# Loading the key weights of a projection by contraction rows instead of by column halves

## The chip, the cores and the metric

The kernel runs on one core of a Trainium2 chip. The metric is the device time of one execution in microseconds (us). Executions of one kernel scatter by about 0.4 us to either side. So two things are read side by side: timed runs, compared with runs of the kernel before on the same chip in the same session, and traces, in which the moment when a given matmul starts can be compared to 0.01 us.

## The reference, cut to what matters

```
x = A_x                                  # 2048 tokens x 1024
g = sigmoid((x * gate_w).sum(-1))
a = linear_attention(x, A_wqkv, A_wo)    # q, k, v = x @ A_wqkv; phi(k) = exp(k) or k + 1; ...
b = sliding_window_attention(x, B_wqkv, B_wo)
return g * a + (1 - g) * b
```

Only the first step matters here: the keys of the linear attention, `k = x @ A_wqkv[:, 1024:2048]`, a product of 2048 tokens by 1024 contraction rows by 1024 columns, followed by `phi`.

## The kernel before

The kernel starts with that product. It hands x to TensorE (PE) transposed, in blocks of 128 contraction rows ("a row", kt, from 0 to 7) by 128 tokens ("a tile", t). The transposed blocks are made by transposing DMAs straight from memory, so at the start every matmul waits for two things: a block of x and a block of weights. The sums of four token tiles by two halves of 512 columns are kept in eight tiles of PSUM (`first` below; "the banks" from here on), and the loop goes over the contraction outside, so that work can begin when a part of the rows is there.

```python
WkA = [wpool.tile([P, KT, 512], BF16, name=f"WkA{h}", tag="wa") for h in range(2)]

def load_xT(k, t0, t1):      # two rows, tiles t0 to t1: 128 KB for two tiles, 256 KB for four
    nc.sync.dma_start_transpose(out=xT[:, 2*k:2*k+2, t0*P:t1*P], in_=rows(x, t0*P, t1*P)[:, 2*k*P:(2*k+2)*P])
def load_wk(eng, k, h):      # two rows, half of the columns: 256 KB in pieces of 1 KB
    eng.dma_start(out=WkA[h][:, 2*k:2*k+2, :], in_=A_wqkv[2*k*P:(2*k+2)*P, D+512*h:D+512*h+512] ...)

load_wk(nc.scalar, 0, 0)
load_xT(0, 0, 2)
load_xT(0, 2, 4)
load_wk(nc.sync, 0, 1)
for k in range(1, 4):
    load_wk(nc.sync, k, 0)
    load_xT(k, 0, 4)
    load_wk(nc.sync, k, 1)
for t in range(4, NB):       # the other twelve token tiles
    nc.sync.dma_start_transpose(out=xT[:, :, t*P:(t+1)*P], in_=rows(x, t*P, (t+1)*P))
# ... other weights
WqA = load_w("WqA", A_wqkv, 0, "wa")        # later, into the space of WkA

warm_up(37)                  # matmuls on constants
first = [bank_k(i) for i in range(8)]
for k in range(4):           # pairs of rows
    for half in range(2):
        for t in range(4):
            for kt in (2*k, 2*k+1):
                project(first[4*half+t], t, kt, half)
            if k == 3:       # the bank is complete: ScalarE and VectorE empty it
                phi(work, pk[:, t, half*512:(half+1)*512], first[4*half+t])
for t in range(4, NB): ...   # 16 matmuls per tile, each bank complete after 8
```

The softmax here doesn't subtract the row's maximum and nothing guards it: scores larger than these inputs give would overflow.

Of the kernel before, what the change touches and what calls it, by code (L numbers as in the profile page):

```python
# [10 lines left out]
BF16 = mybir.dt.bfloat16  # L11
# [3 lines left out]
SP = mybir.EngineType.SP  # L15
P = 128
# [23 lines left out]
def kernel(  # L40
# [11 lines left out]
    nc = tc.nc  # L52
    S, D = A_x.shape[1:]
    assert D == 1024 and S == 2048

    x = A_x[0].rearrange("(m two) d -> two m d", two=2)
    out2 = out[0].rearrange("(m two) d -> two m d", two=2)

    def rows(ap, s0, s1):
        return ap[s0 // 1024, s0 % 1024:(s1 - 1) % 1024 + 1, :]  # L60
# [3 lines left out]
    KT = D // P  # L64
# [4 lines left out]

    consts = ctx.enter_context(tc.tile_pool(name="consts", bufs=1))  # L70
    wpool = ctx.enter_context(tc.tile_pool(name="wpool", bufs=2))
    dram = ctx.enter_context(tc.tile_pool(name="dram", bufs=1, space=bass.MemoryType.DRAM))
    big = ctx.enter_context(tc.tile_pool(name="big", bufs=1))
    ps_pj = ctx.enter_context(tc.tile_pool(name="ps_pj", bufs=4, space=bass.MemoryType.PSUM))

    def load_w(name, src, col0, tag, only=(0, 1)):
        halves = []
        for h in only:
            w = wpool.tile([P, KT, 512], BF16, name=f"{name}{h}", tag=tag)
            c0 = col0 + h * 512  # L80
            nc.sync.dma_start(out=w[:], in_=src[:, c0:c0 + 512].rearrange("(kt p) n -> p kt n", p=P))
            halves.append(w)
        return halves

    xT = big.tile([P, KT, S], BF16, name="xT", tag="xT")
    xrow = big.tile([P, NB, D], BF16, name="xrow", tag="vV")

    def load_rows(eng, t0, t1):
        eng.dma_start(out=xrow[:, t0:t1, :], in_=rows(x, t0 * P, t1 * P).rearrange("(t p) d -> p t d", p=P))

    WkA = [wpool.tile([P, KT, 512], BF16, name=f"WkA{h}", tag="wa") for h in range(2)]

    def load_xT(k, t0, t1):
        nc.sync.dma_start_transpose(out=xT[:, 2 * k:2 * k + 2, t0 * P:t1 * P],  # L94
                                    in_=rows(x, t0 * P, t1 * P)[:, 2 * k * P:(2 * k + 2) * P])

    def load_wk(eng, k, h):
        eng.dma_start(out=WkA[h][:, 2 * k:2 * k + 2, :],  # L98
                      in_=A_wqkv[2 * k * P:(2 * k + 2) * P, D + 512 * h:D + 512 * h + 512]
                      .rearrange("(kt p) n -> p kt n", p=P))  # L100

    ones = nc.const_aps.tensor(1.0, [P, P], BF16)
    with tc.manual_schedule(engines={SP}):
        load_wk(nc.scalar, 0, 0)
        load_xT(0, 0, 2)
        load_xT(0, 2, 4)
        load_wk(nc.sync, 0, 1)
        for k in range(1, 4):
            load_wk(nc.sync, k, 0)
            load_xT(k, 0, 4)  # L110
            load_wk(nc.sync, k, 1)
        for t in range(4, NB):
            nc.sync.dma_start_transpose(out=xT[:, :, t * P:(t + 1) * P], in_=rows(x, t * P, (t + 1) * P))
        for t in range(0, NB, 4):
            load_rows(nc.sync, t, t + 4)
        gw_row = consts.tile([P, D], BF16, name="gw_row")
        nc.sync.dma_start(out=gw_row[:], in_=gate_w.partition_broadcast(P))
        WvA = load_w("WvA", A_wqkv, 2 * D, "wb")
        WoA = load_w("WoA", A_wo, 0, "wo")
        WvB = load_w("WvB", B_wqkv, 2 * D, "wc")  # L120
    WqA = load_w("WqA", A_wqkv, 0, "wa")



# [13 lines left out]
    for slot in range(2):  # L138
        nc.gpsimd.memset(qsel[:, slot:slot + 1], 0.0)
        for pair in range(2):  # L140
            r = 64 * pair + 32 * slot
# [9 lines left out]
    def phi(work, dst, pj):  # L151
        e = work.tile([P, 512], F32, name="e", tag="e")
        nc.scalar.activation(out=e[:], in_=pj[:], func=ACT.Exp)  # L153
        nc.vector.tensor_scalar(out=e[:], in0=e[:], scalar1=1.0, scalar2=1e-6, op0=ALU.min, op1=ALU.add)  # L154
        nc.vector.scalar_tensor_tensor(out=dst, in0=pj[:], scalar=0.0, in1=e[:], op0=ALU.max, op1=ALU.add)

    with tc.manual_schedule(engines={PE}):

        with ExitStack() as s1:
# [4 lines left out]
            s1.enter_context(tc.manual_schedule(engines={DVE}))  # L164
            pk = big.tile([P, NB, D], BF16, name="pk", tag="pkO")
            def project(pj, t, kt, half):
                nc.tensor.matmul(pj[:], lhsT=xT[:, kt, t * P:(t + 1) * P], rhs=WkA[half][:, kt, :],  # L167
                                 start=(kt == 0), stop=(kt == KT - 1))

            def warm_up(n):  # L170
# [7 lines left out]
            def bank_k(i):  # L178
                return (ps_1.tile([P, 512], F32, name="pk1_ps", tag="p1") if i & 4 else
                        ps_pj.tile([P, 512], F32, name="pk_ps", tag="pj"))  # L180

            first = [bank_k(i) for i in range(8)]
            for k in range(4):
                for half in range(2):
                    for t in range(4):
                        for kt in (2 * k, 2 * k + 1):
                            project(first[4 * half + t], t, kt, half)
                        if k == 3:
                            phi(work, pk[:, t, half * 512:(half + 1) * 512], first[4 * half + t])
            for t in range(4, NB):  # L190
                for half in range(2):
                    pj = bank_k(2 * t + half)
                    for kt in range(KT):
                        project(pj, t, kt, half)
                    phi(work, pk[:, t, half * 512:(half + 1) * 512], pj)
# [6 lines left out]
            for t in range(1, NB):  # L202
                side.append(lambda t=t: nc.vector.tensor_tensor(
                    out=zacc[:], in0=zacc[:] if t > 1 else pk[:, 0, :], in1=pk[:, t, :], op=ALU.add))
            side.append(lambda: nc.gpsimd.partition_all_reduce(zrow[:], zacc[:], P, bass_isa.ReduceOp.add))
            for t in range(NB):
                side.append(lambda t=t: nc.vector.tensor_tensor_reduce(
                    out=gjunk[:], in0=xrow[:, t, :], in1=gw_row[:], scale=1.0, scalar=0.0, op0=ALU.mult,
# [3 lines left out]
            for half in range(2):  # L212
                g_ = junk.tile([P, KT, 512], BF16, name=f"G{half}", tag=f"G{half}")
                G.append(g_)
                for kt in range(KT):
                    pj = ps_pj.tile([P, 512], F32, name="g_ps", tag="pj")
                    for t in range(NB):
                        nc.tensor.matmul(pj[:], lhsT=xrow[:, t, kt * P:(kt + 1) * P],  # L218
                                         rhs=pk[:, t, half * 512:(half + 1) * 512],
# [12 lines left out]
            for g in range(2):  # L232
                kvp = ps_pj.tile([P, 512], F32, name="kv_ps", tag="pj")[:, 0:256].rearrange("p (c d) -> p c d", c=4)
                for c in range(4):
                    for kt in range(KT):
                        for j in range(2):
                            cols = slice(c * P + 64 * j, c * P + 64 * j + 64)
                            nc.tensor.matmul(kvp[64 * j:64 * j + 64, c, :], lhsT=WvA[g][:, kt, cols],  # L238
                                             rhs=G[g][:, kt, cols], start=(kt == 0), stop=(kt == KT - 1))
# [85 lines left out]
            def qa_units(t, bank, evacuate):  # L325
                def mm(half, kt, st):
                    if kt == 0:
                        st["pj"] = bank()
                    nc.tensor.matmul(st["pj"][:], lhsT=xT[:, kt, t * P:(t + 1) * P], rhs=WqA[half][:, kt, :],  # L329
                                     start=(kt == 0), stop=(kt == KT - 1))  # L330
                    if kt == KT - 1:
                        evacuate(t, half, st["pj"])
                for half in range(2):
                    st = {}
                    for kt in range(KT):
                        yield lambda half=half, kt=kt, st=st: mm(half, kt, st)
# [23 lines left out]
        with ExitStack() as s2:  # L360
# [158 lines left out]
            for c in range(KT):  # L519
                kts[c] = kpool.tile([P, 2, 1024], BF16, name="kt", tag="kt")  # L520
                for hh in range(2):
# [3 lines left out]
                    if 1 <= c <= 2:  # L525
                        t = 2 * (c - 1) + hh
                        nc.sync.dma_start_transpose(out=pqT[0][:, :, t * P:(t + 1) * P],
                                                    in_=pqd[t * P:(t + 1) * P, :])
# [5 lines left out]
            load_wo(1, 0, 8)  # L534
            raw = wpool.tile([P, 4, D], BF16, name="raw", tag="wc")
            fw = wpool.tile([P, 2, D], F32, name="fw", tag="wc")
            lw = wpool.tile([P, 4, D], BF16, name="lw", tag="wa")

            def qa_output(t, half):
                def lhsT(r, kt, j):  # L540
                    return xT[64 * r:64 * r + 64, kt, t * P + 64 * j:t * P + 64 * j + 64]

                def rhs(r, kt):
                    return WqA[half][64 * r:64 * r + 64, kt, :]

                def evacuate(ps, part):
                    if part == 0:
                        nc.scalar.copy(out=raw[:, t - 12, half * 512:(half + 1) * 512], in_=ps[:])
                return lhsT, rhs, evacuate
# [5 lines left out]
        with ExitStack() as s3:  # L555
# [48 lines left out]
            for i, p_ in enumerate(parts):  # L604
# [4 lines left out]
                f = out_part(i, *p_)  # L609
# [33 lines left out]
```

## Time and profile before

| | before |
|---|---|
| median of the first three runs | 473.69 us |
| span of the traced execution | 472.5 us |
| PE busy | 467.8 us (99%) |
| first projection starts | 4.74 us |
| last wait of PE for a load ends | 9.51 us |
| first matmul of the next stage ("G") | 61.32 us |

The page of the profile: the span, PE's busy time, and the chain of work that ended last, followed back from the end.

```profile
span 472.5 us, 13174 instructions
...
PE 467.8 (99%) x5765; PEld 246.4 (52%) x5765; DVE 277.2 (59%) x601; ACT 169.2 (36%) x272; POOL 15.3 (3%) x30
...
PE 97%; DMA 1%; SPq 1%; ACT 0%; issue 0%
```

PE is the bottleneck from end to end: 97% of the chain. All that anything else can win is the time in which PE waits. The timeline of PE shows where that is (start, duration, engine, line, operation, output and inputs, shapes, count, and in brackets the idle time before it with what ended it):

```profile
3.03 1.91 PE L173 MATMUL warm<-const-bfloat16-1.0 128*128 128x128 bf16 x16
4.74 1.10 PE L167 MATMUL pk_ps<-WkA,xT 128*128 128x512 bf16 x4
6.01 2.80 PE L167 MATMUL pk_ps<-WkA,xT 128*128 128x512 bf16 x12 [0.18 <-DMA xT<-in_A_x_dram]
9.51 12.69 PE L167 MATMUL pk_ps<-WkA,xT 128*128 128x512 bf16 x58 [0.69 <-DMA xT<-in_A_x_dram]
```

L173 is the warm-up, L167 the projection. PE waits for a block of x before 6.01 and before 9.51 us, and never again in this stage. Two cautions for reading: the idle time in brackets is too small, because a matmul is drawn as 0.38 us long while the next one starts 0.216 us after it; and the two idle stretches are better taken from the starts of single matmuls, 5.46 to 6.01 and 8.44 to 9.51 us, which is 0.33 and 0.85 us more than 0.216.

The timeline of the sync queue (SP), which issues the loads. A duration here is the time that issuing takes, not the transfer:

```profile
0.80 2.60 SPq L94 DMA_TRANSPOSE xT<-in_A_x_dram  x2
3.45 1.09 SPq L98 DMA_DIRECT2D WkA<-in_A_wqkv_dram  x2
4.58 1.24 SPq L94 DMA_TRANSPOSE xT<-in_A_x_dram  x1
5.87 1.12 SPq L98 DMA_DIRECT2D WkA<-in_A_wqkv_dram  x2
```

The transposes (L94) took 1.30 and 1.24 us to issue at 128 KB and 1.24, 1.73 and 1.24 us at 256 KB (the last two at 7.03 and 9.95 us, after these lines); the loads (L98) 0.46 to 0.59 us. And what the DMA engines moved in each microsecond (the two columns that matter are the last: their busy share, which is the sum of the packets' times and passes 1 where these overlap, and GB/s):

```profile
1.50:2.50 1.00, 1.00 (x13) 1.00 (x10) 0.00 (x0) 0.58 (x1) 0.32 (x3) 1.00 0.35 69
2.50:3.50 1.00, 1.00 (x12) 1.00 (x11) 0.00 (x0) 0.00 (x0) 0.00 (x0) 1.00 1.03 293
3.50:4.50 1.00, 1.00 (x12) 1.00 (x11) 0.00 (x0) 0.00 (x0) 0.00 (x0) 1.00 0.59 133
4.50:5.50 1.00, 1.00 (x9) 0.54 (x6) 0.00 (x0) 0.00 (x0) 0.00 (x0) 1.00 0.74 127
5.50:6.50 1.00, 0.82 (x5) 0.25 (x4) 0.00 (x0) 0.00 (x0) 0.00 (x0) 1.00 1.04 287
6.50:7.50 1.00, 1.00 (x6) 0.44 (x5) 0.00 (x0) 0.00 (x0) 0.00 (x0) 1.00 1.42 266
7.50:8.50 1.00, 1.00 (x7) 0.39 (x4) 0.00 (x0) 0.00 (x0) 0.00 (x0) 1.00 0.94 113
8.50:9.50 1.00, 0.31 (x2) 0.00 (x0) 0.00 (x0) 0.00 (x0) 0.47 (x2) 1.00 1.06 267
```

Between 3.5 and 5.5 us they move 130 GB/s, in the two microseconds after that 266 to 287.

### The profile page before, as it was taken

The numbers are of one execution on the slowest core, as the hardware profiler recorded it, in microseconds if no ns is written. First come the engines' busy times: TensorE is split into PE (matmuls) and PEld (weight loads), VectorE is DVE, ScalarE is ACT, GpSimd is POOL, SyncE is SP. The second block draws the span as 40 slices with busy tenths as digits, with TensorE's granted clock in tenths as the row PEclk, the third lists the DMA queues.
The fourth block names the chain that finished last, engine by engine and source line by source line (L and its number), as shares of the span: only waits on it lengthen the run. The fifth ranks groups of instructions, "written<-read, shape, count | busy, mean of one in ns | idle before, by whom it ended". The sixth has DMA issues, their size and how long they took to land.

```text
span 472.5 us, 13174 instructions
## 1 busy us (share of the span) xinstructions
PE 467.8 (99%) x5765; PEld 246.4 (52%) x5765; DVE 277.2 (59%) x601; ACT 169.2 (36%) x272; POOL 15.3 (3%) x30
## 2 busy tenths in 40 slices
PE   8999999999999999999999999999999999999997
PEld 5444444445444444445666666666665444444444
DVE  0496689990329999999567676767660039900000
ACT  1343321102543333333555555555551134221122
POOL 3300000500000000000000000000000000000000
PEclk9999999999999999999999999999999999999999
DMA  8999980000643233627326526432563853321101
GB/s 196 211 233 378 349 259 0 0 1 0 214 136 105 92 138 132 154 96 244 109 56 104 112 49 94 101 86 59 92 147 83 163 136 76 70 56 45 34 33 46
DMA packets 98780, 55.40 MB, mean 117 GB/s; under 512 B 70178, under 2 KB 90658, under 8 KB 98722
## 3 DMA queue, kind: packets, MB, share of 16 engines
q1 hardware_dynamic: 93554, 50.10, 41.4%
q10 hardware_dynamic: 5168, 4.46, 3.1%
q8 instruction: 45, 0.74, 0.7%
q14 instruction: 13, 0.11, 0.1%
HBM read 26.10 MB, written 15.86 MB: 89 GB/s over the span
## 4 chain that ended last, share of the span: by engine, by line
PE 97%; DMA 1%; SPq 1%; ACT 0%; issue 0%
PE q_ps L387 27%; PE d_ps L584 12%; PE p_ps L293 12%; PE g_ps L218 12%; PE e_ps L584 12%; PE pk_ps L167 11%; PE p_ps L329 9%; PE po L466 2%; PE s2b L444 2%; DMA xT<-in_A_x_dram 1%; SPq L94 1%; PE kv_ps L238 0%; PE w_ps L281 0%; SPq L98 0%; ACT osb L589 0%
## 5 line engine op out<-in xcount | busy, mean ns | idle before, releaser
L387 PE MATMUL q_ps<-xT,WqB 64*64 64x512 bf16 x1024 | 68.3, 377 | 0.0
L387 PE MATMUL q_ps<-xT,WkB 64*64 64x512 bf16 x1024 | 68.0, 377 | 0.0
L154 DVE TENSOR_SCALAR e<-e 128x512 f32<-128x512 f32 x64 | 27.0, 422 | 65.3 <-ACT e L153 65.3
L293 PE MATMUL p_ps<-WvB,xT 128*128 128x512 bf16 x256 | 57.7, 379 | 0.0
L167 PE MATMUL pk_ps<-WkA,xT 128*128 128x512 bf16 x256 | 55.9, 379 | 0.9 <-DMA xT<-in_A_x_dram 0.9
L218 PE MATMUL g_ps<-pk,xrow 128*128 128x512 bf16 x256 | 55.4, 379 | 0.0
L449 ACT ACTIVATE PT<-s2b 128x928 bf16<-128x928 f32 (+4 forms) x40 | 34.2, 854 | 45.5 <-PE s2b L444 45.5
L451 DVE TENSOR_TENSOR PT<-PT,mask 128x928 bf16<-128x928 bf16 (+4 forms) x40 | 23.6, 590 | 38.2 <-ACT PT L449 38.2
L329 PE MATMUL p_ps<-WqA,xT 128*128 128x512 bf16 x192 | 43.4, 379 | 0.0
L584 PEld LDWEIGHTS <-pqT 128*128 128x128 bf16 x272 | 26.0, 98 | 29.8 <-issue 0.4
L584 PEld LDWEIGHTS <-OBT 128*128 128x128 bf16 x272 | 26.0, 98 | 29.4
L167 PEld LDWEIGHTS <-xT 128*128 128x128 bf16 x256 | 24.8, 98 | 31.5 <-DMA xT<-in_A_x_dram 1.9
L218 PEld LDWEIGHTS <-xrow 128*128 128x128 bf16 x256 | 25.0, 98 | 30.2
L293 PEld LDWEIGHTS <-xT 128*128 128x128 bf16 x256 | 24.7, 98 | 30.2 <-issue 0.9
L387 PEld LDWEIGHTS <-WkB 64*64 64x64 bf16 x1024 | 31.9, 107 | 15.2 <-issue 0.4
L387 PEld LDWEIGHTS <-WqB 64*64 64x64 bf16 x1024 | 31.5, 106 | 15.3 <-issue 0.7
L153 ACT ACTIVATE e<-pk_ps 128x512 f32<-128x512 f32 x32 | 18.9, 597 | 41.1 <-PE pk_ps L167 36.9
L298 ACT CAST tmp<-p_ps 128x512 bf16<-128x512 f32 x32 | 18.8, 589 | 35.5 <-PE p_ps L293 30.1
L584 PE MATMUL d_ps<-WoA,pqT 128*128 128x512 bf16 (+1 forms) x136 | 30.9, 370 | 0.0
L584 PE MATMUL d_ps<-WoB,OBT 128*128 128x512 bf16 (+1 forms) x136 | 30.8, 370 | 0.0
L329 PEld LDWEIGHTS <-xT 128*128 128x128 bf16 x192 | 18.8, 98 | 22.6
L584 PE MATMUL e_ps<-WoA,pqT 128*128 128x512 bf16 (+2 forms) x136 | 30.0, 363 | 0.0
(61 smaller groups left out, 486.9 us busy)
## 6 DMA issues: line engine op xcount, KB each, us to landing
vd<-tmp SPq DMA_DIRECT2D x16, 264.0 KB
xrow<-in_A_x_dram SPq DMA_DIRECT2D x4, 1024.0 KB
out_dram<-osb ACTq DMA_DIRECT2D x31, 128.0 KB
pqd<-tmp SPq DMA_DIRECT2D x12, 256.0 KB
WvA<-in_A_wqkv_dram SPq DMA_DIRECT2D x2, 1024.0 KB
WoA<-in_A_wo_dram SPq DMA_DIRECT2D x2, 1024.0 KB
WvB<-in_B_wqkv_dram SPq DMA_DIRECT2D x2, 1024.0 KB
WqA<-in_A_wqkv_dram SPq DMA_DIRECT2D x2, 1024.0 KB
```

The costliest lines, as they stand in the source:

```text
L153: nc.scalar.activation(out=e[:], in_=pj[:], func=ACT.Exp)
L154: nc.vector.tensor_scalar(out=e[:], in0=e[:], scalar1=1.0, scalar2=1e-6, op0=ALU.min, op1=ALU.add)
L167: nc.tensor.matmul(pj[:], lhsT=xT[:, kt, t * P:(t + 1) * P], rhs=WkA[half][:, kt, :], start=(kt == 0), stop=(kt == KT - 1))
L218: nc.tensor.matmul(pj[:], lhsT=xrow[:, t, kt * P:(kt + 1) * P], rhs=pk[:, t, half * 512:(half + 1) * 512], start=(t == 0), stop=(t == NB - 1))
L293: nc.tensor.matmul(st["pj"][:], lhsT=xT[:, kt, t * P:(t + 1) * P], rhs=WvB[half][:, kt, :], start=(kt == 0), stop=(kt == KT - 1))
L298: nc.scalar.copy(out=v[:, half * 16:(half + 1) * 16, 0:Dh], in_=st["pj"][:].rearrange("p (h e) -> p h e", h=16))
L329: nc.tensor.matmul(st["pj"][:], lhsT=xT[:, kt, t * P:(t + 1) * P], rhs=WqA[half][:, kt, :], start=(kt == 0), stop=(kt == KT - 1))
L387: nc.tensor.matmul(banks[o][64 * j:64 * j + 64, :], lhsT=lhsT(r, kt, j), rhs=rhs(r, kt), start=first and kt == 0, stop=kt == KT - 1, skip_ ...
L444: nc.tensor.matmul(s2b[64 * par:64 * par + 64, pair, :, o:o + w], lhsT=kts[c][r, par, k0:k0 + 64], rhs=qz[r, :, par, q0 % 512:q0 % 512 + w ...
L449: nc.scalar.activation(out=pt[:, :, 0:W_], in_=s2b[:].rearrange("p a b s -> p (a b) s")[:, :, 0:W_], func=ACT.Exp, scale=SCALE)
L451: nc.vector.tensor_tensor(out=pt[:, :, 0:W_], in0=pt[:, :, 0:W_], in1=mask[:, None, base:base + W_].broadcast_to([P, 4, W_]), op=ALU.mult)
L584: nc.tensor.matmul(st["ps"][:, 0:n], lhsT=lhsT, rhs=W[c0 // 512][:, c, c0 % 512:c0 % 512 + n], start=(side == 0 and c == 0), stop=(side == ...
```

## The change

Its intent: PE should begin with all four token tiles and both column halves of one row, so that the first 8 matmuls need the least data. The weights are loaded one row at a time over all 1024 columns (256 KB as before, but in pieces of 2 KB), into one tile; rows 0 and 1 have a transpose each (128 KB), the rest go by pairs (256 KB). The groups follow: rows 0 and 1 alone, then pairs. The queue, with what has to be there before PE can go on:

```
position   before                               changed
1 (ACT)    weights rows 0+1, left half          weights row 0
2          x rows 0+1, tiles 0 and 1            x row 0, four tiles
3          x rows 0+1, tiles 2 and 3            weights row 1
4          weights rows 0+1, right half         x row 1
5          weights rows 2+3, left half          weights row 2
6          x rows 2+3    <- PE goes on          x rows 2+3
7          weights rows 2+3, right half         weights row 3  <- PE goes on
```

```diff
-    WkA = [wpool.tile([P, KT, 512], BF16, name=f"WkA{h}", tag="wa") for h in range(2)]
+    WkA = wide.tile([P, KT, D], BF16, name="WkA", tag="wa")       # wide: a new pool with one buffer
-    def load_xT(k, t0, t1): ...
-    def load_wk(eng, k, h): ...
+    def load_xT(kt, n, t0, t1):
+        nc.sync.dma_start_transpose(out=xT[:, kt:kt + n, t0 * P:t1 * P],
+                                    in_=rows(x, t0 * P, t1 * P)[:, kt * P:(kt + n) * P])
+    def load_wk(eng, kt):
+        eng.dma_start(out=WkA[:, kt, :], in_=A_wqkv[kt * P:(kt + 1) * P, D:2 * D])
 ...
+        load_wk(nc.scalar, 0)
+        load_xT(0, 1, 0, 4)
+        load_wk(nc.sync, 1)
+        load_xT(1, 1, 0, 4)
+        for kt in range(2, KT):
+            load_wk(nc.sync, kt)
+            if kt % 2 == 0:
+                load_xT(kt, 2, 0, 4)
 ...
-    WqA = load_w("WqA", A_wqkv, 0, "wa")
+    WqA = wide.tile([P, KT, D], BF16, name="WqA", tag="wa")       # one DMA of 2 MB instead of two
+    nc.sync.dma_start(out=WqA[:], in_=A_wqkv[:, 0:D].rearrange("(kt p) n -> p kt n", p=P))
 ...
-            for k in range(4):
+            for kts_ in ((0,), (1,), (2, 3), (4, 5), (6, 7)):
                 for half in range(2):
                     for t in range(4):
-                        for kt in (2 * k, 2 * k + 1):
+                        for kt in kts_:
                             project(first[4 * half + t], t, kt, half)
-                        if k == 3:
+                        if kts_[-1] == KT - 1:
                             phi(...)
 ... (the later readers of WqA and the tile lw follow suit)
```

More of the change, by code (lines that the diff above doesn't have):

```diff
@@ L71 @@
     wpool = ctx.enter_context(tc.tile_pool(name="wpool", bufs=2))
+    wide = ctx.enter_context(tc.tile_pool(name="wide", bufs=1))
     dram = ctx.enter_context(tc.tile_pool(name="dram", bufs=1, space=bass.MemoryType.DRAM))
@@ L89, in load_rows @@
         eng.dma_start(out=xrow[:, t0:t1, :], in_=rows(x, t0 * P, t1 * P).rearrange("(t p) d -> p t d", p=P))
-    WkA = [wpool.tile([P, KT, 512], BF16, name=f"WkA{h}", tag="wa") for h in range(2)]
-    def load_xT(k, t0, t1):
-        nc.sync.dma_start_transpose(out=xT[:, 2 * k:2 * k + 2, t0 * P:t1 * P],
-                                    in_=rows(x, t0 * P, t1 * P)[:, 2 * k * P:(2 * k + 2) * P])
-    def load_wk(eng, k, h):
-        eng.dma_start(out=WkA[h][:, 2 * k:2 * k + 2, :],
-                      in_=A_wqkv[2 * k * P:(2 * k + 2) * P, D + 512 * h:D + 512 * h + 512]
-                      .rearrange("(kt p) n -> p kt n", p=P))
-    ones = nc.const_aps.tensor(1.0, [P, P], BF16)
-    with tc.manual_schedule(engines={SP}):
-        load_wk(nc.scalar, 0, 0)
-        load_xT(0, 0, 2)
-        load_xT(0, 2, 4)
-        load_wk(nc.sync, 0, 1)
-        for k in range(1, 4):
-            load_wk(nc.sync, k, 0)
-            load_xT(k, 0, 4)
-            load_wk(nc.sync, k, 1)
+    WkA = wide.tile([P, KT, D], BF16, name="WkA", tag="wa")
[4 more added lines that the diff above has]
+        eng.dma_start(out=WkA[:, kt, :], in_=A_wqkv[kt * P:(kt + 1) * P, D:2 * D])
+    ones = nc.const_aps.tensor(1.0, [P, P], BF16)
+    with tc.manual_schedule(engines={SP, mybir.EngineType.Activation}):
+        load_wk(nc.scalar, 0)
[6 more added lines that the diff above has]
+                load_xT(kt, 2, 0, 4)
         for t in range(4, NB):
@@ L166, in project @@
             def project(pj, t, kt, half):
-                nc.tensor.matmul(pj[:], lhsT=xT[:, kt, t * P:(t + 1) * P], rhs=WkA[half][:, kt, :],
+                nc.tensor.matmul(pj[:], lhsT=xT[:, kt, t * P:(t + 1) * P], rhs=WkA[:, kt, half * 512:half * 512 + 512],
                                  start=(kt == 0), stop=(kt == KT - 1))
@@ L328, in mm @@
                         st["pj"] = bank()
-                    nc.tensor.matmul(st["pj"][:], lhsT=xT[:, kt, t * P:(t + 1) * P], rhs=WqA[half][:, kt, :],
+                    nc.tensor.matmul(st["pj"][:], lhsT=xT[:, kt, t * P:(t + 1) * P], rhs=WqA[:, kt, half * 512:half * 512 + 512],
                                      start=(kt == 0), stop=(kt == KT - 1))
@@ L536 @@
             fw = wpool.tile([P, 2, D], F32, name="fw", tag="wc")
-            lw = wpool.tile([P, 4, D], BF16, name="lw", tag="wa")
+            lw = wide.tile([P, 4, D], BF16, name="lw", tag="wa")
             def qa_output(t, half):
@@ L543, in rhs @@
                 def rhs(r, kt):
-                    return WqA[half][64 * r:64 * r + 64, kt, :]
+                    return WqA[64 * r:64 * r + 64, kt, half * 512:half * 512 + 512]
                 def evacuate(ps, part):
```

## The prediction

> What bounds the kernel. The page gives PE busy 467.8 of 472.5 us (99%), and its chain of waits is 97% PE: every stage is a gapless stream of matmuls. The change neither adds nor removes a matmul (the order of instructions on PE, DVE and ACT is the same after the first 64 projections; the queue issues one DMA fewer, the two 1 MB loads of WqA having become one). It can only pay where PE waits, and that is before 9.51 us.
>
> The start, from the timeline and the trace's completion times. Warm-up matmuls run 0.84 to 4.95 us; the first projection starts at 4.74, just after the first transposed block of x landed (4.68). Then PE waits 0.18 us for the second block (landed 5.97) and 0.69 us for the second k-group's block (9.46). From 9.51 on it never waits: 48 matmuls take 10.53 us, 219 ns each, and the 64 projections of the first four tiles end at 20.04. [...] Without any wait the 64 would end at 4.74 + 64 x 0.219 = 18.8. So 1.3 us, 0.27%, is all that can be won.
>
> What the change does there.
> 1. The first block is one row for all four token tiles: 128 KB as before, so it lands at about 4.7 again. The 8 matmuls of row 0 run 4.7 to 6.5 with no wait (0.18 us saved).
> 2. Row 1 needs its weights and a 128 KB block, issued second and third on the queue. Issue costs 1.24 us per transpose and 0.58 per load; I expect the block at 6.2 to 6.5. Row 1 runs to about 8.3.
> 3. Rows 2 and 3 need weight row 3 for their second matmul already, and that load is issued after the 256 KB block. By then 1.5 MB must have arrived; before, PE could go on after 1.25 MB, because half the columns were enough. This is the bill for loading both column halves together. Against it: weight packets double from 1 to 2 KB. Elsewhere in this trace 1 KB packets move at 350 GB/s and 2 KB packets at 390, so 256 KB takes 0.67 instead of 0.75 us [...]. The queue also idles less between 4.5 and 6 us, where it moved some 150 GB/s. Estimate: block at 8.6, weight row 3 at 9.4 (the same position landed at 10.24).
> 4. So PE waits about 1 us in one place, 8.3 to 9.4, then runs through: weight row 5 (estimate 12.2, needed 13.0) and row 7 (15.0, needed 16.5) are in time. The 64 end at about 9.4 + 47 x 0.219 = 19.7, against 20.04.
>
> Gain: 0.3 to 0.4 us. Later parts are off the path: WqA now waits for the last reader of both key halves (about 62 us instead of 60), but is read only beyond 117 us. lw waits for all WqA readers, which end before it is written.
>
> Predicted: 473.3 us, 472.6 to 474.1. Faster by over 2%: 0.5%; within 2%: 99%; slower: 0.5%.
>
> To be seen if right: PE idle about 1 us in one piece around 8.3 to 9.4, released by a WkA load rather than xT; the 64 end at 19.4 to 20; everything later shifted by the same few tenths.
>
> Wrong if: weight row 3 lands at 10.2 as before (then 0.5 us slower), or weight row 5 after 13 us, a second wait; a better fed queue (row 3 by 8.5) would give up to 1.2 us.

(9.4 + 47 x 0.219 = 19.7 us against 20.04, a gain of 0.3 to 0.4 us, is made of numbers from the trace of before and estimates from them.)

## The result, and the profile after

| | before | changed |
|---|---|---|
| median, first comparison (6 runs each) | 473.80 us | 474.14 us |
| ratio | | 1.0007, interval 0.9994 to 1.002 |
| PE goes on for good (second matmul of rows 2 and 3 in the changed kernel) | 9.51 us | 9.86 us |
| first G matmul | 61.32 us | 61.44 us |

Ratios are the mean time of one kernel's fast runs over that of the other's of the same rounds, so they are not quite the ratios of the medians quoted beside them.

The change is not a gain of 0.4 us but, by the medians, a loss of 0.3. The interval of the ratio holds no change too, so the sign rests on the traces, of which e1, e13, e14, e17 and e20 add more. The page and PE's timeline of the changed kernel, to be read against those of before:

```profile
span 472.3 us, 13141 instructions
...
PE 466.3 (99%) x5735; PEld 244.8 (52%) x5765; DVE 277.3 (59%) x601; ACT 169.1 (36%) x272; POOL 15.3 (3%) x30
...
PE 86%; SPq 11%; DMA 2%; issue 1%; ACT 0%
```

```profile
4.74 4.14 PE L167 MATMUL pk_ps<-WkA,xT 128*128 128x512 bf16 x15
9.19 0.39 PE L167 MATMUL pk_ps<-WkA,xT 128*128 128x512 bf16 x1 [0.31 <-DMA xT<-in_A_x_dram]
9.86 12.46 PE L167 MATMUL pk_ps<-WkA,xT 128*128 128x512 bf16 x56 [0.28 <-DMA WkA<-in_A_wqkv_dram]
```

The start is as planned: 16 matmuls of rows 0 and 1 without a wait for data (one of the 16 records is missing). The first four of them start 0.43, 0.43 and 0.32 us apart instead of 0.216, which costs nothing here because PE has to wait afterwards anyway; e8 and e10 come back to it. Then PE waits twice: until 9.19 us for the x block of rows 2 and 3, does a single matmul, and waits until 9.86 for the weights of row 3. From there it runs through. (The chain now shows SPq with 11%. This is no new wait: 30 matmul records are missing, 5735 of 5765, each leaves a false gap in PE, and at one such gap, at 63.17 us, the walk back leaves PE for a load of WvB and goes along the queue. The trace of e1 lacks as many records and has PE at 97%.)

In the changed kernel the 18th matmul starts at 9.86 us, in the kernel before at 9.73. This lag of 0.12 to 0.13 us is still there, unchanged, at the first G matmul. Nothing else in the first 350 us differs between the two traces by more than 0.02 us; near 353 us the trace of before loses 0.2 us more, which is why its span is the longer one all the same.

The sync queue and the DMA engines:

```profile
0.80 1.26 SPq L95 DMA_TRANSPOSE xT<-in_A_x_dram  x1
2.12 0.56 SPq L99 DMA_DIRECT2D WkA<-in_A_wqkv_dram  x1
2.72 1.15 SPq L95 DMA_TRANSPOSE xT<-in_A_x_dram  x1
3.92 0.58 SPq L99 DMA_DIRECT2D WkA<-in_A_wqkv_dram  x1
4.54 1.35 SPq L95 DMA_TRANSPOSE xT<-in_A_x_dram  x1
5.93 1.05 SPq L99 DMA_DIRECT2D WkA<-in_A_wqkv_dram  x2
```

```profile
1.50:2.50 1.00, 1.00 (x13) 1.00 (x11) 0.00 (x0) 0.58 (x1) 0.32 (x3) 1.00 0.60 86
2.50:3.50 1.00, 1.00 (x12) 1.00 (x11) 0.00 (x0) 0.00 (x0) 0.00 (x0) 1.00 1.11 293
3.50:4.50 1.00, 1.00 (x12) 1.00 (x10) 0.00 (x0) 0.00 (x0) 0.00 (x0) 1.00 0.81 137
4.50:5.50 1.00, 1.00 (x7) 0.53 (x5) 0.00 (x0) 0.00 (x0) 0.00 (x0) 1.00 1.21 243
5.50:6.50 1.00, 1.00 (x5) 0.44 (x4) 0.00 (x0) 0.00 (x0) 0.00 (x0) 1.00 0.97 199
6.50:7.50 1.00, 1.00 (x7) 0.47 (x5) 0.00 (x0) 0.00 (x0) 0.00 (x0) 1.00 1.48 187
7.50:8.50 1.00, 0.95 (x6) 0.41 (x5) 0.00 (x0) 0.00 (x0) 0.00 (x0) 1.00 0.95 230
8.50:9.50 1.00, 0.69 (x3) 0.11 (x2) 0.00 (x0) 0.00 (x0) 0.58 (x2) 1.00 1.08 304
```

The sixth DMA of the kernel is issued from 4.54 us (before: 4.58), the seventh from 5.93 (before: 5.87). And from 1.5 to 7.5 us the engines moved 86 + 293 + 137 + 243 + 199 + 187 = 1145 KB (before: 69 + 293 + 133 + 127 + 287 + 266 = 1175 KB). The stretch from 4.5 to 5.5 us was better filled (243 against 127), and the gain was given back in the next two. From 7.5 to 9.5 us the changed kernel did get ahead: 534 KB against 380, so 1679 against 1555 KB in all. The story in two lines: PE now needs the seventh item where it needed the sixth, and the faster arrival that was to pay for it came only in part.

### The profile page after: what moved, and what is told of

Read it like the earlier page. It is cut to its first block, busy times and chain, and to the rows that moved or that the text cites. A ratio compares the mean times of both kernels' runs of the same rounds, so it can differ in the third digit from the quotient of the medians.

```text
span 472.3 us, 13141 instructions
## 1 busy us (share of the span) xinstructions
PE 466.3 (99%) x5735; PEld 244.8 (52%) x5765; DVE 277.3 (59%) x601; ACT 169.1 (36%) x272; POOL 15.3 (3%) x30
## 4 chain that ended last, share of the span: by engine, by line
PE 86%; SPq 11%; DMA 2%; issue 1%; ACT 0%
PE q_ps L387 27%; PE d_ps L584 12%; PE p_ps L293 12%; PE e_ps L584 11%; PE g_ps L218 11%; PE p_ps L329 9%; SPq L112 4%; SPq L82 4%; DMA WvB<-in_B_wqkv_dram 2%; PE po L466 2%; PE s2b L444 2%; SPq L95 1%; SPq L99 1%; SPq L116 1%; SPq L90 0%
## 5 line engine op out<-in xcount | busy, mean ns | idle before, releaser
L584 PEld LDWEIGHTS <-pqT 128*128 128x128 bf16 x272 | 26.0, 98 | 29.8 <-issue 0.4
L584 PE MATMUL e_ps<-WoB,OBT 128*128 128x512 bf16 (+2 forms) x133 | 29.7, 363 | 0.2
```

What stands on the lines that cost most here:

```text
L584: nc.tensor.matmul(st["ps"][:, 0:n], lhsT=lhsT, rhs=W[c0 // 512][:, c, c0 % 512:c0 % 512 + n], start=(side == 0 and c == 0), stop=(side == ...
```

## The experiments

All changes are made in the changed kernel unless said otherwise. "Landed" is the time when the last of a DMA's completion signals was recorded in the trace; "first G matmul" sums up everything that happened in the start. Every kernel gave correct results.

| run | first G matmul, us | x rows 2+3 / weights row 3 landed, us | median us (before beside it) | ratio, 95% interval |
|---|---|---|---|---|
| before | 61.32 | 9.46 / - | 473.80 | |
| changed | 61.44 | 9.14 / 9.82 | 474.14 (473.80) | 1.0007, 0.9994 to 1.002 |
| e1_repeat | 61.67 | 9.00 / 10.05 | 474.68 (473.90) | 1.0014, 1.0002 to 1.0027 |
| e2_single_rows | 61.23 | 8.97 / 10.62 | 473.88 (473.90) | 0.9997, 0.9984 to 1.0009 |
| e3_weights_first | 63.91 | 10.36 / 9.32 | 474.73 (473.90) | 1.0015, 1.0001 to 1.0028 |
| e5_tile_only | 61.34 | 9.48 / - | 473.48 (473.90) | 0.9993, 0.9980 to 1.0006 |
| e4_act_queue | 63.78 | 7.34 / 10.53 | 476.93 (473.79) | 1.0070, 1.0054 to 1.0087 |
| e6_single_all | 61.34 | 8.79 / 10.66 | 473.99 (473.79) | 1.0006, 0.9994 to 1.0018 |
| e8_rows_act | 63.52 | one block per row | 478.58 (473.79) | 1.0098, 1.0071 to 1.0125 |
| e9_short_packets | 61.52 | 9.03 / 9.77 | 474.69 (473.79) | 1.0020, 1.0007 to 1.0033 |
| e10_pair_last | 60.56 | 8.70 / 10.26 | 473.60 (473.66) | 0.9997, 0.9984 to 1.0010 |
| e11_split_block | 61.24 | one block per row | 473.65 (473.66) | 0.9999, 0.9987 to 1.0011 |
| e12_row1_act | 60.89 | 7.63 / 9.16 | 474.56 (473.66) | 1.0018, 1.0002 to 1.0034 |
| e13_before_copy | 61.15 | 9.30 / - | 473.85 (473.41) | 1.0006, 0.9994 to 1.0019 |
| e16_pair_last2 | 60.93 | 8.88 / 10.78 | 473.57 (473.41) | 1.0002, 0.9989 to 1.0016 |
| e14_before_look | 61.15 | 9.29 / - | one run | |
| e17_changed_look | 61.93 | 8.96 / 10.30 | one run | |
| e20_changed_look2 | 61.37 | 9.08 / 9.75 | one run | |
| e18_short_look | 64.42 | 8.84 / 11.11 | one run | |
| e19_short_look2 | 61.65 | 9.15 / 10.03 | one run | |

(For the kernel before, e5, e13 and e14 the first of the two numbers is the block of x of rows 2 and 3, on which PE goes on there. Single runs are used for their traces alone.)

The theory: PE restarts at the seventh item of the queue instead of the sixth, and the queue is no faster. Rivals: the merged tile or the 2 MB load costs something later; the 2 KB pieces are to blame; the transposes hold the weights up.

### e1_repeat: the changed kernel again

No edit.

> The changed kernel again, unaltered. Theory: the change costs 0.1 us at the start (first G matmul at 61.44 us in its profile against 61.32 before) and nothing later; so the ratio to the kernel before is 1.000 within 0.0007, and the profile again shows two waits of PE, about 0.5 us each, around 8.5 and 9.2 us, the first for the block of x of rows 2 and 3 and the second for weight row 3. Rival: something later, hidden in the profile by scatter, costs 0.3 us or more; then the ratio stays at 1.0007 or above while the first G matmul stays at 61.4.

Measured: ratio 1.0014, first G matmul 61.67 us, two waits at the same places, the second until 10.09 us. The places hold; the size does not: the loss at the start was 0.35 us here, against 0.12 in the first trace, and the timed ratio lies outside the 0.0007 expected. So the landing of weight row 3 scatters, and one trace is not enough. The rival is not ruled out by this run alone (e5 and the traces of e13 and after bear on it).

### e5_tile_only: the tiles without the loads

The kernel before, with the one-tile WkA, the single load of WqA and the new pool; loads and groups of the start are those of before.

```diff
-    WkA = [wpool.tile([P, KT, 512], ...) for h in range(2)]
+    WkA = wide.tile([P, KT, D], BF16, name="WkA", tag="wa")
-        eng.dma_start(out=WkA[h][:, 2 * k:2 * k + 2, :], ...
+        eng.dma_start(out=WkA[:, 2 * k:2 * k + 2, 512 * h:512 * h + 512], ...
     ... (WqA and lw as in the changed kernel)
```

> The kernel before with only the tiles changed: the key weights in one tile, WqA loaded by one DMA, lw in the same pool; loads and groups of the start as in the kernel before. Theory (all of the effect is in the start's loads and groups): as before, first G matmul at 61.3, ratio 1.000 within 0.0007. Rival (the merged tile or the single 2 MB load costs later): start as before but the ratio at 1.0007 or above.

Measured: first G matmul 61.34 us (before 61.32), the block of x at 9.48 us (before 9.46), ratio 0.9993. The merged tile and the late 2 MB load cost nothing that this comparison can see (interval 0.9980 to 1.0006); the effect is in the loads and groups of the start.

### e2_single_rows: rows 2 and 3 one after the other

```diff
-for kts_ in ((0,), (1,), (2, 3), (4, 5), (6, 7)):
+for kts_ in ((0,), (1,), (2,), (3,), (4, 5), (6, 7)):
```

> The changed kernel, with rows 2 and 3 as two groups of one row. Theory (the wait for weight row 3 at the second matmul of the pair is the loss): the second wait goes, PE restarts at the landing of the x block, about 9.2 us, and runs through; first G matmul 0.25 us earlier than in the changed kernel, at about 61.2 us (0.1 us earlier than in the kernel before). Rival (the order inside the group does not matter, the queue only moves the wait): a new wait for weight row 3 after row 2, first G matmul at 61.4.

Measured: the second wait is gone from its place; a shorter one came two rows later, at the second matmul of rows 4 and 5:

```profile
4.74 3.71 PE L167 MATMUL pk_ps<-WkA,xT 128*128 128x512 bf16 x15
9.02 3.84 PE L167 MATMUL pk_ps<-WkA,xT 128*128 128x512 bf16 x17 [0.58 <-DMA xT<-in_A_x_dram]
13.10 8.14 PE L167 MATMUL pk_ps<-WkA,xT 128*128 128x512 bf16 x36 [0.23 <-DMA WkA<-in_A_wqkv_dram]
```

First G matmul 61.23 us, 0.21 before the changed kernel's first trace and 0.44 before its second, with weight row 3 landing later than in either (10.62 us). So that landing was harmless as soon as nobody waited for it at 9.2 us. The rival was half right: a wait did move on, but to weight row 5 and at 0.23 us by the bracket.

### e3_weights_first: the weights ahead of the block of x

```diff
-            if kt % 2 == 0:
-                load_xT(kt, 2, 0, 4)
+            if kt % 2 == 1:
+                load_xT(kt - 1, 2, 0, 4)
```

> The changed kernel, with weight row 3 (and 5 and 7) issued ahead of the x block of its pair. Theory (1.5 MB must have arrived whichever comes last): one wait instead of two, for the x block, until about 9.8 us; first G matmul at 61.45 to 61.7. Rival (what is late is the weight load itself, behind the slow transposed packets): restart by 9.2 us, first G matmul at 61.2 or below.

Measured: a single wait at rows 2 and 3, for the block of x, which as the seventh item landed at 10.36 us, later than expected; by the timed runs (ratio 1.0015) this order is no better than the changed kernel's. As far as this one trace shows, position in the queue matters, not the kind of item. (The "slow" of the rival, in the trace of before: the transposes alone moved 188 to 197 GB/s from 20 to 29.8 us, the plain loads 347 to 403 from 33 to 60 us.) (PE also waited 0.33 us by the bracket for the x block of row 1, because it had begun earlier in this execution, at 4.25 us.) The first G matmul at 63.91 us is in part an accident of the traced execution (477.06 us; the five others took 474.44 to 475.02): PE stood idle for 2.04 us by the bracket, and from 10.47 us on the granted clock was at half (0.51 between 10.4 and 13.8 us, 0.99 in the 3.4 us after that), about 1.7 us lost; without that the first G matmul would have come at about 62.2 (estimate from these two). The same thing was caught again in e18, where the table shows it.

### e4_act_queue: the weights from a second queue

```diff
-        load_wk(nc.sync, 1)
+        load_wk(nc.scalar, 1)
-            load_wk(nc.sync, kt)
+            load_wk(nc.scalar, kt)
```

> The changed kernel with all eight loads of WkA issued by ACT's queue and only the transposes by the sync queue; groups and tiles as in the changed kernel. Theory A (between 3.5 and 7 us the DMA engines are short of work because one queue issues everything, 0.6 us per load and 1.3 us per transpose): with two queues issuing, the x block of rows 2 and 3 lands by 8.0 us and weight row 3 by 8.5; PE waits under 0.4 us in all, first G matmul at 60.4 to 60.8 us. Theory B (the engines are busy, packets are slow): the same 1.5 MB arrive at the same time, weight row 3 or the x block lands at 9.5 us or later, because weights of later rows now take a share; first G matmul at 61.3 or later.

Measured: both theories were partly right, and the kernel was worse than either said. The engines had been short of work, and with two queues issuing they were not; the DMA columns of the same two microseconds, in which the changed kernel had 137 and 243 GB/s:

```profile
3.50:4.50 1.00, 1.00 (x12) 1.00 (x11) 0.00 (x0) 0.00 (x0) 0.00 (x0) 1.00 1.08 367
4.50:5.50 1.00, 0.78 (x6) 0.31 (x4) 0.00 (x0) 0.00 (x0) 0.00 (x0) 1.00 1.13 291
```

In the six microseconds 1527 KB came instead of 1145, and the block of x of rows 2 and 3 landed at 7.34 us. But what came was not what PE needed next. The timeline merges seven of the ACT queue's loads into one line of 11.12 us from 0.83 us, 1.59 us for each in the mean, against 0.46 to 0.59 us for a load on the sync queue of the kernel before; what held them back is not shown by this view. The sync queue, free of the weights, had issued its five transposes by 7.51 us and ran ahead to the blocks of the other twelve tiles (from 7.56 us). Weight row 3 landed at 10.53 us, and PE waited for weights three times:

```profile
5.17 4.08 PE L167 MATMUL pk_ps<-WkA,xT 128*128 128x512 bf16 x16 [0.22 <-DMA xT<-in_A_x_dram]
10.57 3.61 PE L167 MATMUL pk_ps<-WkA,xT 128*128 128x512 bf16 x16 [1.33 <-DMA WkA<-in_A_wqkv_dram]
14.75 3.61 PE L167 MATMUL pk_ps<-WkA,xT 128*128 128x512 bf16 x16 [0.57 <-DMA WkA<-in_A_wqkv_dram]
19.11 5.12 PE L167 MATMUL pk_ps<-WkA,xT 128*128 128x512 bf16 x22 [0.75 <-DMA WkA<-in_A_wqkv_dram]
```

The time is 3 us worse. Here the order of arrival was worth more than the pace.

### e8_rows_act: one transpose per row, weights from the second queue

As e4, with single rows throughout and a transpose for each.

```diff
-            if kt % 2 == 0:
-                load_xT(kt, 2, 0, 4)
+            load_xT(kt, 1, 0, 4)
```

> Every row a group of its own, one transpose per row, loads of WkA issued by ACT's queue. If the engines are starved by the issue (A): each row's 384 KB are there before PE needs them, about every 1.75 us; no wait after the first landing, first G matmul at 60.1 to 60.4 us, ratio about 0.997. If the engines' packets are slow (B): rows come every 1.7 to 1.8 us after a late row 1, waits of 0.1 to 0.5 us for several rows; first G matmul at 60.6 to 61.2.

A miss for both: ratio 1.0098, first G matmul at 63.52 us. The first block of x landed at 5.75 us instead of 4.31, so PE began late. But from then on it waited for no load:

```profile
5.79 15.93 PE L166 MATMUL pk_ps<-WkA,xT 128*128 128x512 bf16 x62 [0.85 <-DMA xT<-in_A_x_dram]
```

What cost time was the rate: until 9.9 us ten matmuls followed each other every 0.43 us (the first and last a little faster) instead of 0.216, and the 65th waited for VectorE, as in e6 below. The sum closes: without any delay the 65th would start at 4.74 + 64 x 0.216 = 18.56 us; the late start adds 1.05, the slow matmuls 1.95, the wait 0.53, and it started at 22.09. The spacing of 0.43 us is that measured in e18 while the granted clock was 0.50; the trace's first record of the granted clock is at 9.77 us here and at 5.79 in the changed kernel, so the PEclk column says nothing before that. Why it comes late here was not tested. The trace is of the fastest run: the times scatter from 476.26 to 480.39 us; the two slowest (480.23 and 480.39) have a mean granted clock of 0.996, as the run of e3 with the long idle. It was not followed further.

### e6_single_all: every row a group of its own

```diff
-for kts_ in ((0,), (1,), (2, 3), (4, 5), (6, 7)):
+for kts_ in ((0,), (1,), (2,), (3,), (4,), (5,), (6,), (7,)):
```

> The changed kernel's loads with every one of the eight rows a group of its own. Theory: both second-matmul waits (weight rows 3 and 5) go; PE waits once, for the x block of rows 2 and 3, till 9.0 to 9.2 us, and runs through; first G matmul at 61.0 to 61.15 us, ratio 0.9985 to 0.9997. Rival (the waits move on to other rows): first G matmul at 61.2 or later.

Measured: by the 40th matmul PE was 0.50 us ahead of the kernel before, as the theory has it. At the 65th, the first of the ninth tile half, it lost 0.52 us at once:

```profile
19.90 15.27 PE L167 MATMUL pk_ps<-WkA,xT 128*128 128x512 bf16 x69 [0.36 <-DVE pk L155]
```

A new wait, for VectorE (L155 is the last step of `phi`, which frees a bank). With a single row last, all eight banks become complete within 8 x 0.216 = 1.7 us; with a pair last, one every 0.43 us from 3.5 us before the end. `phi` costs 0.60 us on ScalarE, then 0.42 and 0.69 on VectorE, so the first bank is free about 1.7 us after it is complete: too late for the ninth tile half, which wants it right away. Gain turned into a new wait. Neither theory had seen this.

### e10_pair_last and e16_pair_last2: single rows, but a pair at the end

```diff
-for kts_ in ((0,), (1,), (2, 3), (4, 5), (6, 7)):
+for kts_ in ((0,), (1,), (2,), (3,), (4,), (5,), (6, 7)):
```

> The changed kernel's loads; rows 0 to 5 each a group of its own, rows 6 and 7 as a pair. Theory: what the all-single version won at the start (0.5 us by the 40th matmul) it lost at the 65th to 68th because with a single last row all eight banks end within 1.7 us and VectorE frees the first too late; with the pair last the wait of 0.4 us on VectorE is gone and the win stays: first G matmul at 60.8 to 61.0 us, ratio 0.9985 to 0.9995. Rival (VectorE is the limit whatever the order): wait stays, first G matmul at 61.3.

> The version with rows 0 to 5 single and 6 and 7 paired, once more. Theory from its first trace: first G matmul at 60.6 to 61.0 us. If the gain of 0.76 us that its first trace showed is real against a typical run of the kernel before: ratio 0.9982 to 0.9990. If the trace of the kernel before was a slow one: ratio 0.9990 to 1.0000, as in the first timing (0.9997).

Measured: the wait for VectorE is gone, and so is every wait for a load in e10; PE's timeline is one piece:

```profile
4.74 19.51 PE L167 MATMUL pk_ps<-WkA,xT 128*128 128x512 bf16 x87
```

One piece is weaker evidence than it looks, because the drawn length of 0.38 us hides a short wait: the timeline of e16 is one piece too, and yet by the starts of its matmuls PE waited 0.28 us for the block of x (until 8.93) and 0.15 us for weight row 3 (until 10.82). In e10 there is no such step, in part by luck: its first three matmuls came more slowly than 0.216 us apart, so that PE was ready for row 2 only at 8.76 us (4.74 + 16 x 0.216 would be 8.20), just after the block had landed (8.70).

First G matmul 60.56 and 60.93 us, in the mean 0.46 us before the mean of three traces of the kernel before (61.32, 61.15, 61.15). The timings don't show it: 0.9997 and 1.0002, each with an interval of 0.0013 to either side, that is 0.6 us. A gain of 0.46 us (0.9990) lies inside both intervals, and so does none at all. The step from the changed kernel to this one is 0.1% by the ratios (1.0007 and 1.0014 against 0.9997 and 1.0002), as large as the intervals, and the runs are of different sessions; it is shown by the traces only (61.60 us in the mean of four against 60.56 and 60.93).

### e11_split_block: a transpose each for rows 2 and 3

As e10, with

```diff
-            if kt % 2 == 0:
+            if kt < 4:
+                load_xT(kt, 1, 0, 4)
+            elif kt % 2 == 0:
                 load_xT(kt, 2, 0, 4)
```

> As the version with the pair last, and the x block of rows 2 and 3 as two transposes of one row each, so that row 2 needs 128 KB less. If arrival is ordered by bytes: row 2's block lands 0.6 us sooner, at 8.2 to 8.5; row 3 then waits for its block until about 10.2 (needed at 10.0), first G matmul at 60.5 to 60.9. If the extra transpose (1.3 us of issue, late in the queue) costs more than the split gains: a wait at row 3 or 4 of over 0.5 us, first G matmul at 61.0 or later.

Measured: the extra transpose costs more than the split gains. The block of row 2 landed 0.38 us earlier than the block of rows 2 and 3 in e10 (8.32 against 8.70), but PE was busy with rows 0 and 1 and began row 2 at the same time (8.75 against 8.76); and everything behind was issued a transpose later: a wait of 0.52 us for the block of rows 4 and 5 at 12.88 us, first G matmul at 61.24 us.

### e12_row1_act: one load more from the second queue

As e10, with weight row 1 issued by ACT right behind row 0.

```diff
-        load_wk(nc.sync, 1)
+        load_wk(nc.scalar, 1)
```

> As the version with the pair last, and weight row 1 issued by ACT's queue right behind row 0. If the sync queue's issue is what leaves the engines short of work between 3.5 and 5.5 us: everything behind lands 0.4 to 0.6 us earlier, the x block of rows 2 and 3 at 8.3 to 8.6, first G matmul at 60.3 to 60.6, if the first block of x is not pushed beyond 4.8 us by the load beside it. If the engines' own pace is the limit: the first block of x comes at 4.8 us or later and the x block of rows 2 and 3 at 8.8 to 9.1 as before; first G matmul at 60.8 to 61.1.

Measured: half of each. The block of x of rows 2 and 3 is issued from 4.04 us instead of 4.51 and lands at 7.63 us instead of 8.70: the issue did pace the queue. But the load beside it pushed the first block of x from 4.17 to 5.53 us, and PE stood still at the very start, then ran through:

```profile
5.57 18.79 PE L167 MATMUL pk_ps<-WkA,xT 128*128 128x512 bf16 x86 [0.63 <-DMA xT<-in_A_x_dram]
```

First G matmul 60.89 us. The runs fall into two kinds, 473.49 to 473.76 and 475.36 to 475.60 us, three each; no trace fell on the slow kind, so its cause is open. (Slow first matmuls after a late start, as in e8 with 0.43 us, are a candidate that no trace of e12 tests.)

### e9_short_packets, e18_short_look, e19_short_look2: 1 KB pieces

The changed kernel, with WkA laid out half by half, so that each row of a load is two runs of 1 KB; same loads, order and groups.

```diff
-    WkA = wide.tile([P, KT, D], BF16, name="WkA", tag="wa")
+    WkA = wide.tile([P, 2, KT, 512], BF16, name="WkA", tag="wa")
-        eng.dma_start(out=WkA[:, kt, :], in_=A_wqkv[kt * P:(kt + 1) * P, D:2 * D])
+        eng.dma_start(out=WkA[:, :, kt, :], in_=A_wqkv[...].rearrange("p (h n) -> p h n", h=2))
```

> The changed kernel, with WkA laid out half by half in its tile, so that the same loads move in 1 KB pieces instead of 2 KB; same issues, order, groups. If 2 KB packets help at the start as they do later (390 against 350 GB/s), four weight rows take 0.3 us longer: weight row 3 lands at 10.1 to 10.4 us and the first G matmul comes at 61.7 to 62.0. If packet size does not matter there: 61.4 to 61.7 as in the changed kernel. If long packets are bad at the start: below 61.4.

> The changed kernel with 1 KB pieces, a second trace. If 2 KB packets are what makes one of the 16 engines late with weight row 3 (first to last engine 0.13 to 1.35 us apart in seven traces of 2 KB loads, 0.12 to 0.19 in four of 1 KB): first to last within 0.2 us again and row 3 at 9.7 to 9.9 us, first G matmul at 61.3 to 61.6. If it is chance: row 3 anywhere from 9.7 to 10.7, spread over 0.5.

> As the second trace of it: spread within 0.2 us and row 3 at 9.7 to 9.9 if 2 KB packets cause the late engine; otherwise anywhere from 9.7 to 10.7.

Measured: weight row 3 landed at 9.77, 10.03 and 11.11 us; with 2 KB pieces (four traces of the changed kernel) at 9.82, 10.05, 10.30 and 9.75, and in four more with the same loads and other groups (e2, e6, e10, e16) at 10.62, 10.66, 10.26 and 10.78. The timed run (474.69 us) equals the repeat of the changed kernel (474.68). The size of the pieces is no gain at the start, and no cause of the late ones either: my suspicion that 2 KB pieces make one engine late fell with e18, where the first of the 16 completions of row 3 came at 9.44 us and the last at 11.11 with 1 KB pieces.

In e18 a slow stretch came after a long wait. PE stood idle for 1.88 us by the bracket, until 11.15, and from 12.12 us on the granted clock (PEclk, the third column from the right) was 0.50 for 3.4 us:

```profile
5.30:8.70 3.40, 3.33 (x16) 1.28 (x14) 0.00 (x0) 0.00 (x0) 0.00 (x0) 1.00 1.05 222
8.70:12.10 3.40, 1.34 (x6) 0.59 (x7) 0.00 (x0) 0.00 (x0) 2.51 (x6) 1.00 1.16 188
12.10:15.50 3.40, 3.40 (x10) 1.23 (x9) 0.00 (x0) 0.00 (x0) 3.22 (x9) 0.50 1.16 319
15.50:18.90 3.40, 3.40 (x18) 1.49 (x16) 0.00 (x0) 0.00 (x0) 1.11 (x7) 0.99 1.06 205
```

The matmuls in that stretch follow each other every 0.43 us instead of 0.216, which cost another 1.7 us on top of the wait (first G matmul 53.27 us after PE went on, against 51.58 in the changed kernel). e3 had the same after an idle of 2.04 us. In e4, with an idle of 1.33 us, the granted clock was 1.00 in every stretch read from 9.5 to 16 us. The mean granted clock of the traced executions is 0.996 in e3 and e18 and 0.999 or 1.000 in all others. Whether the idle caused the fall was not tested.

### e13_before_copy, e14_before_look, e17_changed_look, e20_changed_look2: more traces of the two kernels

No edits.

> The kernel before against itself: the noise of the comparison, and a second trace of it. If its first trace is typical: PE restarts for good at 9.4 to 9.6 us, first G matmul at 61.2 to 61.4, span 472.3 to 472.6. If that trace was a slow one (its execution took 474.2 us, its other runs 473.7): restart at 8.9 to 9.2, first G matmul at 60.8 to 61.1, and then the change costs 0.5 us at the start and not 0.1 to 0.35.

> The kernel before, a third trace: as for the copy of it that is timed. The two together say whether the block of x of the second k-group lands at 9.5 us each time (first trace 9.46, the same loads with the tiles merged 9.48) or earlier as a rule.

> The changed kernel, a third trace. Theory: weight row 3 lands at 9.8 to 10.7 us (five traces of the same loads so far: 9.82, 10.05, 10.62, 10.66, 10.26), so first G matmul at 61.4 to 62.3 us, that is 0.1 to 1 us behind the kernel before; the scatter of that one landing is the scatter of its times.

> The changed kernel, a fourth trace beside them on the same chip: row 3 at 9.8 to 10.7 us, first to last engine 0.1 to 1.3 us apart, first G matmul at 61.4 to 62.3.

Measured: the kernel before against a copy of itself gave 1.0006 with an interval of 0.0013 to either side: a ratio of the size of the result is within the noise of one comparison. The traces are sharper. First G matmul, before: 61.32, 61.15, 61.15, mean 61.21 us; changed: 61.44, 61.67, 61.93, 61.37, mean 61.60 us. The first trace of before was slow by 0.17 us against the two others, not by the 0.3 to 0.5 I had thought possible. The cost at the start is 0.39 us in the mean. The landing on which PE goes on accounts for all of it: from the 17th matmul of before the first G matmul follows after 51.81 us in all three traces, from the 18th of the changed kernel after 51.58 us in all four, and one matmul more lies between. The two timings say 0.07% and 0.14%, or 0.33 and 0.66 us. They agree with it, and no further cost is needed. In e17 and e20 another 0.6 to 0.8 us was lost after the start of the G stage, in e17 0.45 of it in one idle stretch at 353 us that the trace puts down to no wait. I took it for scatter: the first trace of before loses 0.2 us at the same place, and e2, e5, e6, e9 and e10, which have the merged tile and the 2 MB load too, lose nothing there. Its cause is open.

## Why the prediction was wrong

The predicted time was 473.3 us with a range up to 474.1; the median was 474.14. (That it lies 0.04 us outside the range is chance at this scatter; the direction and the step below are what matters.) The class (within 2%) and the bounds of the game (PE busy 99%, at most 1.3 us to be won) held. The direction did not: a gain of 0.3 to 0.4 us was predicted, a loss of about that size came.

- Right: the matmuls are the same, only the first 10 us matter, later parts are off the path (e5: 61.34 against 61.32 us, ratio 0.9993). Rows 0 and 1 run without a wait for data. PE then waits for weight row 3 because both halves of a row now come together; this "bill" was named in step 3, and e2 confirms it: without the need, 0.2 to 0.4 us come back (one trace of e2 against two of the changed kernel).
- Slightly off: the wait came in two pieces with one matmul between them, not one.
- Wrong, and decisive: the term of step 3 in which the queue gets faster. "Estimate: block at 8.6, weight row 3 at 9.4 (the same position landed at 10.24)." Measured in the four traces of the changed kernel: block at 9.14, 9.00, 8.96, 9.08, weight row 3 at 9.82, 10.05, 10.30, 9.75, mean 9.98. The seventh item of the kernel before landed at 10.24, 10.06 and 10.05 in its three traces, mean 10.12. The gain was 0.14 us and not 0.84, and with the four other traces of the same loads (e2, e6, e10, e16; mean of all eight 10.28) there was none. The prediction had two reasons for it, and neither carried. "The queue also idles less between 4.5 and 6 us": it did (243 against 127 GB/s), but by 7.5 us the sum was the same, 1145 against 1175 KB, and the sixth and seventh item were issued at the same moments as before. What the queue gained came later and was lost at the end of the load: the first of the 16 completions of weight row 3 came at 9.69, 9.54, 9.50 and 9.62 us, 0.41 us earlier in the mean than that of the seventh item before (10.11, 9.94, 9.93), but the last of them came 0.13, 0.51, 0.80 and 0.13 us after the first (before: 0.12 to 0.13), and 1.0 to 1.35 us after it in e2, e6, e10 and e16. Why single completions come late is open. And the 2 KB pieces were worth nothing here (e9, e19), though they are worth 390 against 350 GB/s in the long loads from 32 us on.
- The falsifier was written down: "Wrong if: weight row 3 lands at 10.2 as before (then 0.5 us slower)". That is nearly what happened: the seventh item of before landed 0.77 us after the sixth, one matmul (0.216) is done meanwhile, which leaves 0.55 us, and less the 0.14 us gained about 0.4 (measured: 0.39). It had been given too little weight: the estimate of an arrival was trusted to 0.3 us when arrivals of the same load scatter by 0.5 us and more between executions.

What the pace comes from is shown in part. The time to issue is not small here: 1.15 to 1.30 us for a 128 KB transpose in the first traces of the two kernels, and e12 (0.47 us less of issue ahead of it, the block 1.07 us earlier than in e10) and e4 (291 to 367 GB/s instead of 137 to 243) show that one queue leaves the engines short of work between 3.5 and 5.5 us. Why their packets are slow right after, between 5.5 and 7.5 us, with the busy share near or above 1 at 187 to 199 GB/s, stays open.

## What to carry to other kernels

When loads come from one queue in order, name for each wait the position of the last item it needs; a change that keeps the issue times but moves a need from the sixth to the seventh item costs up to one item's time (here 0.77 us, of which 0.39 were lost in the end), and other bytes or pieces have to win that back first. Order the groups of work by single items while data is short, but check the end of the group too: the all-single version gave its 0.5 us back (e6) because all eight banks became complete within 1.7 us and the first was free only about 1.7 us after it was complete. And where the whole effect is a landing that scatters by half a microsecond, take several traces and a copy of the old kernel before believing either sign.
